# Channel attention with a guessed gate: first gate from 44 rows instead of 135, four slots of 68 rows instead of a ring of 45-row tiles, 512-wide sums, and the first two tiles loaded through two queues

## The chip, the cores and the metric

The kernel runs on one core of a Trainium2 chip. The metric is the device time of one execution in microseconds. The kernel before takes 532.75 us, the median of three runs (532.3 to 534.75).

## The reference

A channel attention of the ECA kind, on an image of 384 x 384 places with 384 channels in bfloat16. Its convolution over channels has the width 1, so the gate of a channel depends on that channel's mean alone:

```python
H = W = 384
C = 384
k = 1
"x": normal(1, H, W, C) * 0.05        # bfloat16
"w1d": normal(k) * 0.05

g = jnp.einsum("bhwc->bc", x) / (H * W)
s = _sigmoid(g * w1d[0])
return x * s[:, None, None, :]
```

The mean needs all of x before the first output could be written. x has 113.25 MB, and so has the output.

## The kernel before

**Tiling.** The 147,456 places are spread over 128 partitions, so that there are 1152 "rows", each of 384 channels in all 128 partitions (128 x 768 bytes). They are cut into 26 tiles, eight of 45 rows and eighteen of 44 (`split(n_rows, TILE)`, TILE = 45). A tile is one DMA in and one DMA out, in which each partition moves one contiguous piece of 45 or 44 x 768 bytes. SBUF holds an arena of rows; a ring hands out places in it, and about six tiles fit at once.

**The guess.** Instead of reading x twice, the kernel guesses the gate. It sums the first three tiles (135 rows), makes the gate `s_early` from their mean, and multiplies and stores every tile with it. Meanwhile it goes on summing. At the end it makes the true gate `s_true` from the sum of everything and compares both as bfloat16 bit patterns. If one channel differs, a second pass reads x again and does everything with `s_true`; if none differs, the output already is what it should be.

**The engines.** Each engine has a list of its own that it works through in order; a small planner records the operations, and adds a semaphore wait wherever one needs another's rows or results.

- SP issues all loads (L91). The load of a tile waits until the stores of the tiles whose place it takes have landed (the wait is at L99).
- PE sums (L206): for each row one matmul of a 128 x 128 block of ones with the row's 384 columns, which adds up over the partitions, and over the rows in one PSUM bank. The sums of the first three tiles are in bank 0, all others in bank 1; bank 2 is for the weight (L183), whose one product is scaled by 1/n twice (L192), for the early and the true mean.
- VectorE copies bank 0 to `total` (L249), and gates tile after tile in place (L165). A gate waits for PE, which must have read the tile.
- ACT loads the weight at the start, makes `s_early` (L255), and then issues all stores (L91), each when its gate is done.
- At the end VectorE adds bank 1 to `total` (L267), ACT makes `s_true` (L273), VectorE compares (L281), reduces (L289) and casts to the flag `redo` (L295). SP, ACT and VectorE read the flag (L326) and skip the second pass or run it. ACT waits last for all stores.

The order around the change is made by one loop over the tiles: before a load is recorded, the tiles that stand in its place are "put" (gate and store), then the load, then the sums; `s_early` is recorded behind the sums of the third tile.

Of the kernel before, what the change touches and what calls it, by code (L numbers as in the profile page):

```python
# [3 lines left out]
P = 128  # L4
ROW = 384
BF16 = mybir.dt.bfloat16
F32 = mybir.dt.float32
U16 = mybir.dt.uint16
I32 = mybir.dt.int32
ACT_F = mybir.ActivationFunctionType  # L10
ALU = mybir.AluOpType


class Planner:
# [9 lines left out]
    def __init__(self, nc, name, n_dma_sems):  # L24
        self.nc = nc
        self.streams = {e: [] for e in ("sync", "scalar", "vector", "tensor", "gpsimd")}
        self.sems = {e: nc.alloc_semaphore(f"{name}_{e}") for e in self.COMPUTE}
        self.count = {e: 0 for e in self.COMPUTE}
        self.pool = [nc.alloc_semaphore(f"{name}_dma_{i}") for i in range(n_dma_sems)]
        self.pool_uses = [0] * n_dma_sems  # L30
        self.n_dma = 0
        self.writer = {}
        self.readers = {}
        self.seen = {e: {} for e in self.streams}
        self.final = []
# [70 lines left out]
def split(n, most):  # L106
    k = -(-n // most)
    return [n // k + (i < n % k) for i in range(k)]


class Ring:


    def __init__(self, size):
        self.size, self.at = size, 0

    def take(self, n):
        if self.at + n > self.size:
            self.at = 0
        self.at += n  # L120
        return self.at - n


TILE = 45
AHEAD_TILES = 3


def bass_standalone__channel_attn_eca__vision_kernel(
# [3 lines left out]
    out: bass.AP,  # L132
):
    B, H, W, C = x.shape
    assert B == 1 and C == ROW and (B * H * W) % P == 0
    n_rows = B * H * W // P
    x_rows, o_rows = x.flatten_outer_dims(), out.flatten_outer_dims()

    def dram(view, r0, n):
        return view[r0 * P : (r0 + n) * P, :].rearrange("(p t) c -> p (t c)", p=P)  # L140

    ones = nc.alloc_sbuf_tensor("ones", [P, P], BF16)
    s_early = nc.alloc_sbuf_tensor("s_early", [P, C], BF16)
    s_true = nc.alloc_sbuf_tensor("s_true", [P, C], BF16)
    w_one = nc.alloc_sbuf_tensor("w_one", [1, 16], BF16)
    w_scaled = nc.alloc_sbuf_tensor("w_scaled", [P, 2], F32)
    warm = nc.alloc_sbuf_tensor("warm", [P, 2], F32)
    wrong = nc.alloc_sbuf_tensor("wrong", [P, 1], F32)
    redo = nc.alloc_sbuf_tensor("redo", [P, 1], I32)
    total = nc.alloc_sbuf_tensor("total", [P, C], F32)  # L150
    n_arena = nc.sbuf_bytes_remaining // (2 * C)
    arena = nc.alloc_sbuf_tensor("arena", [P, n_arena * C], BF16)
    acc = [nc.alloc_psum_tensor(f"acc{i}", [P, 512], F32) for i in range(3)]

    def at(r0, n):
        assert r0 + n <= n_arena
        return arena[:, r0 * C : (r0 + n) * C]

    def rows(r0, n):
        return [("sb", r) for r in range(r0, r0 + n)]  # L160

    def gate(place, n, s):
        s_b = s[:].unsqueeze(1).broadcast_to([P, n, C])
        v = at(place, n).rearrange("p (t c) -> p t c", t=n)
        return lambda e: e.tensor_tensor(v, v, s_b, ALU.mult)  # L165

    sizes = split(n_rows, TILE)
    early_rows = sum(sizes[:AHEAD_TILES])
    plan = Planner(nc, "a", 50)


    plan.op("gpsimd", lambda e: e.memset(warm[:, 0:1], 0.0), writes=["warm"])  # L172
    plan.op("vector", lambda e: e.memset(ones[:], 1.0), writes=["ones"])  # L173
    plan.dma("scalar", w_one[0:1, 0:1], w1d.unsqueeze(0), writes=["w_one"])
    plan.op(
        "scalar",
        lambda e: e.activation(warm[:, 1:2], warm[:, 0:1], ACT_F.Sigmoid),  # L177
        reads=["warm"],
        writes=["warm1"],
    )  # L180
    plan.op(
        "tensor",
        lambda e: e.matmul(  # L183
            acc[2][:, 0:1], ones[0:1, :], w_one[0:1, 0:1], start=True, stop=True
        ),
        reads=["ones", "w_one"],
        writes=["acc2"],
    )
    for i, n in enumerate((early_rows, n_rows)):
        plan.op(  # L190
            "vector",
            lambda e, i=i, n=n: e.tensor_scalar_mul(  # L192
                w_scaled[:, i : i + 1], acc[2][:, 0:1], 1.0 / float(P * n)
            ),
            reads=["acc2"],
            writes=[f"w_scaled{i}"],
        )

    def load(place, n, r0):
        plan.dma("sync", at(place, n), dram(x_rows, r0, n), writes=rows(place, n))  # L200

    def add_rows(place, n, bank, first, last):
        for i in range(n):
            plan.op(
                "tensor",
                lambda e, i=i: e.matmul(  # L206
                    acc[bank][:, :C],
                    ones[:],
                    at(place + i, 1),
                    start=first and i == 0,  # L210
                    stop=last and i == n - 1,
                ),
                reads=["ones"] + (rows(place, n) if i in (0, n - 1) else []),
                writes=[f"acc{bank}"],
                signal=i == n - 1,
            )

    def put(place, n, r0):
        plan.op(
            "vector",  # L220
            gate(place, n, s_early),
            reads=["s_early"] + rows(place, n),
            writes=rows(place, n),
        )
        plan.final.append(
            plan.dma("scalar", dram(o_rows, r0, n), at(place, n), reads=rows(place, n))
        )


    ring = Ring(n_arena)  # L230
    inside = []
    r0 = 0
    for k, n in enumerate(sizes):
        place = ring.take(n)
        while inside and any(
            p < place + n and place < p + m for p, m, _ in inside
        ):
            put(*inside.pop(0))
        load(place, n, r0)
        inside.append((place, n, r0))  # L240
        if k < AHEAD_TILES:
            add_rows(place, n, 0, k == 0, k == AHEAD_TILES - 1)
        else:
            add_rows(place, n, 1, k == AHEAD_TILES, k == len(sizes) - 1)
        r0 += n
        if k == AHEAD_TILES - 1:
            plan.op(
                "vector",
                lambda e: e.tensor_copy(total[:], acc[0][:, :C]),  # L249
                reads=["acc0"],  # L250
                writes=["total"],
            )
            plan.op(
                "scalar",
                lambda e: e.activation(  # L255
                    s_early[:], total[:], ACT_F.Sigmoid, scale=w_scaled[:, 0:1]
                ),
                reads=["total", "w_scaled0", "warm1"],
                writes=["s_early"],
            )  # L260
    for tile in inside:
        put(*tile)


    plan.op(
        "vector",
        lambda e: e.tensor_tensor(total[:], total[:], acc[1][:, :C], ALU.add),  # L267
        reads=["total", "acc1"],
        writes=["total"],
    )  # L270
    plan.op(
        "scalar",
        lambda e: e.activation(  # L273
# [2 lines left out]
        reads=["total", "w_scaled1"],  # L276
        writes=["s_true"],
# [6 lines left out]
        reads=["s_true", "s_early"],  # L284
        writes=["total"],
# [4 lines left out]
        reads=["total"],  # L290
        writes=["wrong"],
# [4 lines left out]
        reads=["wrong"],  # L296
        writes=["redo"],
# [2 lines left out]


    again = Planner(nc, "b", 50)
    ring = Ring(n_arena)
    r0 = 0
    for n in sizes:
        place = ring.take(n)
        again.dma("sync", at(place, n), dram(x_rows, r0, n), writes=rows(place, n))
        again.op(
            "vector",
            gate(place, n, s_true),  # L310
            reads=rows(place, n),
            writes=rows(place, n),
        )
        again.final.append(
            again.dma("scalar", dram(o_rows, r0, n), at(place, n), reads=rows(place, n))
        )
        r0 += n
# [70 lines left out]
```

## Time and profile before

| what | before |
|---|---|
| median of 3 runs | 532.75 us |
| the profiled execution, its own time | 532.74 us |
| its span, from first to last instruction | 530.9 us |
| TensorE busy / VectorE busy | 241.9 / 236.8 us |
| s_early made at | 45.1 us |
| first store issued at | 55.0 us |
| last load issued at | 455.7 us |
| last gate done at | 501.1 us |
| granted TensorE clock, mean | 0.736 |

These are the groups that the change touches. The columns are line, engine, operation, output from inputs, sizes and count, then busy time in us and mean ns of one, then the idle time of the engine just before, and what ended most of it.

```profile
L206 PE MATMUL acc<-arena,ones 128*128 128x384 bf16 x1152 | 241.8, 381 | 248.1 <-DMA arena<-in_x_dram 248.1
L165 DVE TENSOR_TENSOR arena<-arena,s_early 128x16896 bf16<-128x16896 bf16 (+1 forms) x26 | 234.1, 9019 | 222.0 <-PE acc L206 221.3
L249 DVE COPY total<-acc 128x384 f32<-128x384 f32 x1 | 0.6, 557 | 42.1 <-PE acc L206 42.1
L255 ACT ACTIVATE s_early<-total,w_scaled 128x384 bf16<-128x384 f32 x1 | 0.6, 614 | 42.4 <-DVE total L249 42.4
```

And these are the transfers: line, queue, count, size of one, and the median time from its issue to its landing.

```profile
arena<-in_x_dram SPq DMA_DIRECT2D x18, 4224.0 KB, 27.6
out_dram<-arena ACTq DMA_DIRECT2D x18, 4224.0 KB, 73.6
arena<-in_x_dram SPq DMA_DIRECT2D x8, 4320.0 KB, 30.2
out_dram<-arena ACTq DMA_DIRECT2D x8, 4320.0 KB, 58.7
```

PE's idle time is ended by loads and VectorE's by PE: both engines follow the data. A store is on its way for about 3.7 times as long as a turn of 20 us takes, which says that several stores stand in their queue at any time.

### The profile page before, as it was taken

What the parts mean: (1) busy time and instruction counts of PE and PEld (TensorE: products, weight loads), DVE (VectorE), ACT (ScalarE), POOL (GpSimd) and SP (SyncE); (2) the same over time, 40 slices, a digit from 0 to 9 for tenths busy, and PEclk for the clock granted to TensorE, in tenths of its full rate; (3) what the DMA queues carried; (4) which work ended last, traced back from release to release, by engine and by line L of the source; (5) the groups of instructions that cost most, each with busy time, mean ns of one, the idle gap of its engine ahead of it and who ended that gap; (6) DMA issues with size and microseconds to landing.
All of it is one profiled execution on the core that took longest, in us unless ns stands there. A gap on an engine that the chain in (4) does not pass through costs nothing.

```text
span 530.9 us, 2501 instructions
## 1 busy us (share of the span) xinstructions
PE 241.9 (46%) x1153; PEld 127.3 (24%) x1153; DVE 236.8 (45%) x34; ACT 2.7 (1%) x4; POOL 0.3 (0%) x5
## 2 busy tenths in 40 slices
PE   0979643326257256156156266256155265265000
PEld 0435312213123133023033133123033033133000
DVE  0005999561542642642642633642642633633800
ACT  1000000000000000000000000000000000000000
POOL 0000000000000000000000000000000000000000
PEclk9989867588576677686786775686786786676755
DMA  9999999999999999999999999999999999999996
GB/s 372 419 436 437 413 419 440 432 424 442 422 442 422 443 426 438 438 420 444 425 433 446 415 442 440 418 440 437 423 443 428 430 444 415 443 443 414 443 435 290
DMA packets 7502, 226.67 MB, mean 427 GB/s; under 512 B 834, under 2 KB 834, under 8 KB 834
## 3 DMA queue, kind: packets, MB, share of 16 engines
q1 hardware_dynamic: 3744, 113.25, 49.7%
q10 hardware_dynamic: 3746, 113.25, 49.5%
q8 instruction: 9, 0.15, 0.1%
q14 instruction: 3, 0.02, 0.0%
HBM read 113.25 MB, written 113.25 MB: 427 GB/s over the span
## 4 chain that ended last, share of the span: by engine, by line
another core or an unknown queue 63%; DMA 19%; DVE 7%; PE 3%; SPq 1%; issue 1%; ACT 0%; DVEq 0%
DMA arena<-in_x_dram 12%; DMA out_dram<-arena 8%; DVE arena L165 7%; PE acc L206 3%; SPq L91 1%; ACT s_true L273 0%; ACT s_early L255 0%; DVE total L281 0%; DVE total L249 0%; DVE wrong L289 0%; DVE total L267 0%; SPq L99 0%; DVE redo L295 0%; DVEq L99 0%
## 5 line engine op out<-in xcount | busy, mean ns | idle before, releaser
L206 PE MATMUL acc<-arena,ones 128*128 128x384 bf16 x1152 | 241.8, 381 | 248.1 <-DMA arena<-in_x_dram 248.1
L165 DVE TENSOR_TENSOR arena<-arena,s_early 128x16896 bf16<-128x16896 bf16 (+1 forms) x26 | 234.1, 9019 | 222.0 <-PE acc L206 221.3
L206 PEld LDWEIGHTS acc<-arena,ones 128*128 128x128 bf16 x1152 | 127.2, 112 | 362.3 <-DMA arena<-in_x_dram 257.8
L249 DVE COPY total<-acc 128x384 f32<-128x384 f32 x1 | 0.6, 557 | 42.1 <-PE acc L206 42.1
L273 ACT ACTIVATE s_true<-total,w_scaled 128x384 bf16<-128x384 f32 x1 | 0.6, 614 | 455.9 <-DVE total L267 455.9
L177 ACT ACT_TABLE_LOAD x1 | 1.3, 1283 | 1.3 <-PEq L373 1.3
L183 PE MATMUL acc<-w_one,ones 1*128 1x1 bf16 x1 | 0.2, 158 | 2.1 <-DMA w_one<-in_w1d_dram 2.1
L281 DVE TENSOR_TENSOR total<-s_true,s_early 128x384 f32<-128x384 uint16 x1 | 0.6, 559 | 0.7 <-ACT s_true L273 0.7
L255 ACT ACTIVATE s_early<-total,w_scaled 128x384 bf16<-128x384 f32 x1 | 0.6, 614 | 42.4 <-DVE total L249 42.4
L192 DVE TENSOR_SCALAR w_scaled<-acc 128x1 f32<-128x1 f32 x2 | 0.2, 154 | 1.3 <-PE acc L183 1.3
L183 PEld LDWEIGHTS acc<-w_one,ones 1*128 1x128 bf16 x1 | 0.1, 97 | 2.0 <-issue 2.0
L289 DVE TENSOR_REDUCE wrong<-total 128x1 f32<-128x384 f32 x1 | 0.6, 553 | 0.0
L267 DVE TENSOR_TENSOR total<-total,acc 128x384 f32<-128x384 f32 x1 | 0.5, 547 | 0.0
L173 DVE MEMSET ones<- 128x128 bf16 x1 | 0.2, 165 | 0.8 <-PEq L373 0.8
L177 ACT ACTIVATE warm<-warm 128x1 f32<-128x1 f32 x1 | 0.2, 202 | 0.0
L295 DVE CAST redo<-wrong 128x1 int32<-128x1 f32 x1 | 0.2, 154 | 0.0
L373 POOL MEMSET const-bfloat16-1.0<- 128x1 bf16 x1 | 0.1, 103 | 0.0
L373 POOL MEMSET const-uint8-127<- 128x1 uint8 x1 | 0.1, 103 | 0.0
L373 POOL MEMSET const-float32-1.0<- 128x1 f32 x1 | 0.1, 100 | 0.0
L172 POOL MEMSET warm<- 128x1 f32 x1 | 0.1, 99 | 0.3 <-POOLq L373 0.3
L373 POOL MEMSET const-float32-0.0<- 128x1 f32 x1 | 0.1, 99 | 0.2 <-issue 0.2
## 6 DMA issues: line engine op xcount, KB each, us to landing
arena<-in_x_dram SPq DMA_DIRECT2D x18, 4224.0 KB, 27.6
out_dram<-arena ACTq DMA_DIRECT2D x18, 4224.0 KB, 73.6
arena<-in_x_dram SPq DMA_DIRECT2D x8, 4320.0 KB, 30.2
out_dram<-arena ACTq DMA_DIRECT2D x8, 4320.0 KB, 58.7
w_one<-in_w1d_dram ACTq DMA_DIRECT2D x1, 0.0 KB
```

The costliest lines, as they stand in the source:

```text
L91: ("op", lambda e: e.dma_start(out, in_), self.pool[i], 16)
L165: return lambda e: e.tensor_tensor(v, v, s_b, ALU.mult)
L177: lambda e: e.activation(warm[:, 1:2], warm[:, 0:1], ACT_F.Sigmoid),
L183: lambda e: e.matmul(acc[2][:, 0:1], ones[0:1, :], w_one[0:1, 0:1], start=True, stop=True),
L206: lambda e, i=i: e.matmul(acc[bank][:, :C], ones[:], at(place + i, 1), start=first and i == 0, stop=last and i == n - 1,),
L249: lambda e: e.tensor_copy(total[:], acc[0][:, :C]),
L255: lambda e: e.activation(s_early[:], total[:], ACT_F.Sigmoid, scale=w_scaled[:, 0:1]),
L267: lambda e: e.tensor_tensor(total[:], total[:], acc[1][:, :C], ALU.add),
L273: lambda e: e.activation(s_true[:], total[:], ACT_F.Sigmoid, scale=w_scaled[:, 1:2]),
L281: lambda e: e.tensor_tensor(total[:], s_true[:].bitcast(U16), s_early[:].bitcast(U16), ALU.not_equal),
L289: lambda e: e.reduce_max(wrong[:], total[:], axis=mybir.AxisListType.X),
L373: nc = _bacc.Bacc("TRN2", target_bir_lowering=False, num_devices=1)
```

## The change

It has four parts.

1. The early gate is made from the first tile alone, which has 44 rows (EDGE).
2. The ring is replaced by four fixed slots of 68 rows (SLOT). The tiles are one of 44 rows, fifteen of 68, and two of 44 at the end: 18 instead of 26. Tile k stands in slot k mod 4, and its load waits for the store of tile k - 4.
3. A matmul takes 512 columns, a row and a third, instead of 384, and three PSUM banks take turns. Since 512 is 384 + 128, the channels stand shifted by 0, 128 and 256 columns in the three banks; six operations of VectorE add the pieces into `total`, once for the early and once for the full sum.
4. The first two tiles are loaded in two halves by rows, the first half issued by SP and the second by ACT. The loading of the weight moves behind the first tile's load, so that in ACT's list stand: half of tile 0, the weight, `s_early`, half of tile 1, then the stores.

The core of the diff:

```diff
-TILE = 45
-AHEAD_TILES = 3
+WIDE = 512
+EDGE, SLOT = 44, 68
...
-    sizes = split(n_rows, TILE)
-    early_rows = sum(sizes[:AHEAD_TILES])
+    n_slots = n_arena // SLOT
+    full, rest = divmod(n_rows - EDGE, SLOT)
+    if rest < EDGE:
+        full, rest = full - 1, rest + SLOT
+    sizes = [EDGE] + [SLOT] * full + [4 * q for q in split(rest // 4, EDGE // 4)]
...
-    def load(place, n, r0):
-        plan.dma("sync", at(place, n), dram(x_rows, r0, n), writes=rows(place, n))
+    def load(place, n, r0, queues=("sync",)):
+        of = dram(x_rows, r0, n)
+        i = 0
+        for queue, m in zip(queues, split(n, -(-n // len(queues)))):
+            plan.dma(
+                queue,
+                at(place + i, m),
+                of[:, i * C : (i + m) * C],
+                writes=rows(place + i, m),
+            )
+            i += m
...
+    def add_rows(place, n, group, first, last):
+        n_wide = n * C // WIDE
+        start = place * C
+        for i in range(n_wide):
+            bank = acc[group][i % 3]
             plan.op(
                 "tensor",
-                lambda e, i=i: e.matmul(
-                    acc[bank][:, :C],
+                lambda e, i=i, bank=bank: e.matmul(
+                    bank[:, :],
                     ones[:],
-                    at(place + i, 1),
+                    arena[:, start + i * WIDE : start + (i + 1) * WIDE],
...
+    def add_banks(group, copy):
+        for m, lo, hi in ((0, 0, C), (0, C, WIDE), (1, 0, 256), (1, 256, WIDE),
+                          (2, 0, P), (2, P, WIDE)):
+            c = (128 * m + lo) % C
+            part = total[:, c : c + hi - lo]
+            of = acc[group][m][:, lo:hi]
...
-    ring = Ring(n_arena)
     for k, n in enumerate(sizes):
-        place = ring.take(n)
-        while inside and any(
-            p < place + n and place < p + m for p, m, _ in inside
-        ):
+        place = k % n_slots * SLOT
+        if len(inside) == n_slots:
             put(*inside.pop(0))
-        load(place, n, r0)
+        load(place, n, r0, ("sync", "scalar") if k < 2 else ("sync",))
         inside.append((place, n, r0))
-        if k < AHEAD_TILES:
-            add_rows(place, n, 0, k == 0, k == AHEAD_TILES - 1)
+        if k == 0:
+            weight()
+            add_rows(place, n, 0, True, True)
         else:
-            add_rows(place, n, 1, k == AHEAD_TILES, k == len(sizes) - 1)
+            add_rows(place, n, 1, k == 1, k == len(sizes) - 1)
...
-        if k == AHEAD_TILES - 1:
+        if k == 0:
+            add_banks(0, copy=True)
...
+    add_banks(1, copy=False)
```

In the program made from it, PE runs 864 sums where it ran 1152, VectorE 12 adding operations where it ran 2, SP issues 18 loads and ACT 2 where SP issued 26, and ACT issues 18 stores where it issued 26. `weight()` holds the weight's load, the warming of the sigmoid table, the weight's matmul and its two scalings, as they stood at the start before.

More of the change, by code (lines that the diff above doesn't have):

```diff
@@ L108, in split @@
     return [n // k + (i < n % k) for i in range(k)]
[L111 to L121, printed above, removed]
-TILE = 45
-AHEAD_TILES = 3
+WIDE = 512
+EDGE, SLOT = 44, 68
 def bass_standalone__channel_attn_eca__vision_kernel(
@@ L134, in bass_standalone__channel_attn_eca__vision_kernel @@
     B, H, W, C = x.shape
-    assert B == 1 and C == ROW and (B * H * W) % P == 0
+    assert B == 1 and C == ROW and (B * H * W) % (4 * P) == 0
     n_rows = B * H * W // P
@@ L152, in bass_standalone__channel_attn_eca__vision_kernel @@
     arena = nc.alloc_sbuf_tensor("arena", [P, n_arena * C], BF16)
-    acc = [nc.alloc_psum_tensor(f"acc{i}", [P, 512], F32) for i in range(3)]
+    acc = [
+        [nc.alloc_psum_tensor(f"acc{g}_{i}", [P, WIDE], F32) for i in range(3)]
+        for g in range(2)
+    ]
+    w_all = nc.alloc_psum_tensor("w_all", [P, WIDE], F32)
     def at(r0, n):
@@ L165, in gate @@
         return lambda e: e.tensor_tensor(v, v, s_b, ALU.mult)
-    sizes = split(n_rows, TILE)
-    early_rows = sum(sizes[:AHEAD_TILES])
+    n_slots = n_arena // SLOT
[3 more added lines that the diff above has]
+    sizes = [EDGE] + [SLOT] * full + [4 * q for q in split(rest // 4, EDGE // 4)]
+    assert sum(sizes) == n_rows and max(sizes) <= SLOT
     plan = Planner(nc, "a", 50)
@@ L173, in bass_standalone__channel_attn_eca__vision_kernel @@
     plan.op("vector", lambda e: e.memset(ones[:], 1.0), writes=["ones"])
[L174 to L197, printed above, removed]
-    def load(place, n, r0):
-        plan.dma("sync", at(place, n), dram(x_rows, r0, n), writes=rows(place, n))
-    def add_rows(place, n, bank, first, last):
-        for i in range(n):
+    def load(place, n, r0, queues=("sync",)):
[9 more added lines that the diff above has]
+            i += m
@@ L204, in add_rows @@
+    def add_rows(place, n, group, first, last):
[3 more added lines that the diff above has]
+            bank = acc[group][i % 3]
             plan.op(
                 "tensor",
-                lambda e, i=i: e.matmul(
-                    acc[bank][:, :C],
+                lambda e, i=i, bank=bank: e.matmul(
+                    bank[:, :],
                     ones[:],
-                    at(place + i, 1),
-                    start=first and i == 0,
-                    stop=last and i == n - 1,
-                ),
@@ L213, in add_rows @@
-                reads=["ones"] + (rows(place, n) if i in (0, n - 1) else []),
-                writes=[f"acc{bank}"],
-                signal=i == n - 1,
-            )
+                    arena[:, start + i * WIDE : start + (i + 1) * WIDE],
+                    start=first and i < 3,
+                    stop=last and i >= n_wide - 3,
+                ),
+                reads=["ones"] + (rows(place, n) if i in (0, n_wide - 1) else []),
+                writes=[f"acc{group}"],
+                signal=i == n_wide - 1,
+            )
@@ new lines, in add_banks @@
+    def add_banks(group, copy):
[4 more added lines that the diff above has]
+            of = acc[group][m][:, lo:hi]
+            if copy and (m, lo) == (0, 0):
+                emit = lambda e, part=part, of=of: e.tensor_copy(part, of)
+            else:
+                emit = lambda e, part=part, of=of: e.tensor_tensor(
+                    part, part, of, ALU.add
+                )
+            plan.op("vector", emit, reads=[f"acc{group}", "total"], writes=["total"])
@@ L227, in put, with weight @@
         )
-    ring = Ring(n_arena)
+    def weight():
+        plan.dma("scalar", w_one[0:1, 0:1], w1d.unsqueeze(0), writes=["w_one"])
+        plan.op(
+            "scalar",
+            lambda e: e.activation(warm[:, 1:2], warm[:, 0:1], ACT_F.Sigmoid),
+            reads=["warm"],
+            writes=["warm1"],
+        )
+        plan.op(
+            "tensor",
+            lambda e: e.matmul(
+                w_all[:, 0:1], ones[0:1, :], w_one[0:1, 0:1], start=True, stop=True
+            ),
+            reads=["ones", "w_one"],
+            writes=["w_all"],
+        )
+        for i, n in enumerate((sizes[0], n_rows)):
+            plan.op(
+                "vector",
+                lambda e, i=i, n=n: e.tensor_scalar_mul(
+                    w_scaled[:, i : i + 1], w_all[:, 0:1], 1.0 / float(P * n)
+                ),
+                reads=["w_all"],
+                writes=[f"w_scaled{i}"],
+            )
     inside = []
@@ L233, in bass_standalone__channel_attn_eca__vision_kernel @@
     for k, n in enumerate(sizes):
-        place = ring.take(n)
-        while inside and any(
-            p < place + n and place < p + m for p, m, _ in inside
-        ):
+        place = k % n_slots * SLOT
+        if len(inside) == n_slots:
             put(*inside.pop(0))
-        load(place, n, r0)
+        load(place, n, r0, ("sync", "scalar") if k < 2 else ("sync",))
         inside.append((place, n, r0))
-        if k < AHEAD_TILES:
-            add_rows(place, n, 0, k == 0, k == AHEAD_TILES - 1)
+        if k == 0:
+            weight()
+            add_rows(place, n, 0, True, True)
         else:
-            add_rows(place, n, 1, k == AHEAD_TILES, k == len(sizes) - 1)
+            add_rows(place, n, 1, k == 1, k == len(sizes) - 1)
         r0 += n
-        if k == AHEAD_TILES - 1:
[L247 to L252, printed above, removed]
+        if k == 0:
+            add_banks(0, copy=True)
             plan.op(
@@ L262, in bass_standalone__channel_attn_eca__vision_kernel @@
         put(*tile)
[L265 to L270, printed above, removed]
+    add_banks(1, copy=False)
     plan.op(
@@ L302, in bass_standalone__channel_attn_eca__vision_kernel @@
     again = Planner(nc, "b", 50)
-    ring = Ring(n_arena)
     r0 = 0
-    for n in sizes:
-        place = ring.take(n)
+    for k, n in enumerate(sizes):
+        place = k % n_slots * SLOT
         again.dma("sync", at(place, n), dram(x_rows, r0, n), writes=rows(place, n))
```

## The prediction

> **What bounds the kernel now.** I read four views in this order: the busy shares by engine, the 40 slices, the chain of waits, and a table of stages. The first two say what is not the bound and what is.
>
> ```profile
> PE 241.9 (46%) x1153; PEld 127.3 (24%) x1153; DVE 236.8 (45%) x34; ACT 2.7 (1%) x4; POOL 0.3 (0%) x5
> ...
> DMA  9999999999999999999999999999999999999996
> GB/s 372 419 436 437 413 419 440 432 424 442 422 442 422 443 426 438 438 420 444 425 433 446 415 442 440 418 440 437 423 443 428 430 444 415 443 443 414 443 435 290
> ...
> HBM read 113.25 MB, written 113.25 MB: 427 GB/s over the span
> ```
>
> TensorE and VectorE idle more than half of the span; the 16 DMA engines are at nine tenths or more in every slice but the last. Each byte goes in once and out once, so there was one pass. The table of stages (microseconds, busy time of PE, PEld, DVE, ACT, POOL, granted clock, DMA share, GB/s) shows how flat the rate is:
>
> ```profile
> 5.00:45.00 40.00, 26.46 (x135) 14.28 (x135) 0.45 (x1) 0.00 (x0) 0.00 (x0) 0.96 1.02 438
> 45.00:60.00 15.00, 11.65 (x61) 6.40 (x62) 14.32 (x3) 0.61 (x1) 0.00 (x0) 0.89 1.01 415
> 60.00:80.00 20.00, 10.72 (x49) 5.51 (x48) 20.00 (x3) 0.00 (x0) 0.00 (x0) 0.75 0.98 422
> 100.00:480.00 380.00, 179.55 (x838) 93.73 (x838) 168.31 (x20) 0.00 (x0) 0.00 (x0) 0.72 1.00 433
> 480.00:525.00 45.00, 8.76 (x44) 4.72 (x44) 13.29 (x6) 0.61 (x1) 0.00 (x0) 0.61 1.01 433
> 525.00:531.00 6.00, 0.00 (x0) 0.00 (x0) 0.00 (x0) 0.00 (x0) 0.00 (x0) 0.50 0.29 124
> ```
>
> Loads alone (5 to 45), both directions (100 to 480) and stores alone (480 to 525) run at one rate within the counting error of whole packets. So it does not matter when stores begin: 226.5 MB at 433 GB/s are 523 us, and only gaps, overhead per packet and the two ends can be changed. Of the chain, one turn suffices:
>
> ```profile
> 375.76 0.02 issue
> 375.77 0.02 SPq L99
> 375.79 0.03 issue
> 375.82 0.33 SPq L91
> 376.15 19.58 another core or an unknown queue
> ```
>
> SP waits for a store to land (L99), issues the next load (L91), and waits 19.6 us for the next store: a turn of 19.97 us moves 88 rows (a row being 128 x 768 bytes), 0.227 us a row. Stores are far behind when they are issued (median 73.6 us to landing), so the store queue never empties and no engine's slowness is seen.
>
> The DMA packet records of the same trace give finer numbers. A packet of 33,792 bytes starts 1.247 us after the one before on its engine, one of 34,560 bytes 1.275 us: 768 bytes cost 28.2 ns, so a packet has about 4.9 ns that don't grow with it, and a packet followed by a semaphore write costs 6 ns more. With both queues filled, load and store packets alternate one for one. A transfer that joins a queue waits for about three packets already taken (the first store, issued at 54.98, first moves at 59.42); on idle engines the first packet comes 1.0 us after the issue (0.73 to 1.73), and the first packets take about 2.2 us, not 1.28. The engines drift apart: the last store lands between 526.37 and 530.39, a spread of 4.0 us. Beside the 1.4 us steps of the drift lie instruction fetches, nine of 16 KB.
>
> **What the Trainium skill says.** DMA: Bandwidth & Descriptors, section "Issuing engines are not separate DMA queues": transfers from several engines run on the same 16 DMA engines and interleave, and a second issuer saves only the time of issuing. Its section "Queues, rings and completion order" has the engines take turns between queues, a packet each; the one-for-one alternation agrees. TensorE: Matmul & The Clock Gate, section "Wait — 56ns, not 53.3ns?": a 512-wide matmul starts every 426.7 ns cold and 215.7 ns warm; here 384 columns go at 320 ns cold and 166 ns warm, the same price per column. Runtime: NRT & Kernel Launch, section "Instruction fetch mechanics": instructions come in blocks of 16 KiB, 256 each; 1153 matmuls with as many weight loads are 2306 instructions, nine blocks, as the trace has.
>
> **The change part by part.** *Matmuls.* 864 of 512 columns for 1152 of 384: the same columns, so PE keeps about 242 us and stays hidden. It drops 576 instructions with the weight loads, so seven fetches for nine. A fetch holds one DMA engine about 1.4 us, and counts only if that engine ends last: between -2.8 and 0 us.
>
> *Tiles.* 18 for 26. Per DMA engine there were 26 x 2 x 8 = 416 packets; now 18 stores and 16 whole loads x 8, and two loads in halves x 16, make 304. 112 x 4.9 ns = 0.55 us, with 14 fewer semaphore writes 0.63 us saved. The packets grow to 52,224 bytes, a size the trace lacks; above it I take the same slope. If it were 1% worse the whole would be 5 us slower; two sizes with one slope speak against it, so I keep nothing of that.
>
> *Start.* Tile 0 is 22 rows on SP and 22 on ACT, at once, sharing the engines: 44 rows, 10 us, landed at about 13, as the 45 rows of before. The weight's two bytes now queue behind ACT's half and cost 1 us more, since the matmul of the weight stands ahead of tile 0's on PE: start at 14.5. 33 matmuls partly cold, about 9.8 us as tile 0 took before: 24.3. Instead of one copy (0.56) VectorE makes six moves out of PSUM, 384, 128, 256, 256, 128 and 384 columns wide. At the 0.55 us for 384, of which 0.15 is fixed (the one-column operations), they come to 2.4 us; with waits 2.7. With the sigmoid's 0.61 s_early stands at about 27.7, not 45.8. All of this is beside loads already issued.
>
> On ACT the second half of tile 1's load is issued only behind s_early, at 27.8, and store 0 behind that. Tile 1 is therefore complete only at about 55: 34-row packets alternating with SP's 68-row packets, after three taken packets. PE needs 13.7 us (51 matmuls, the first 5 us cold), VectorE 26,112 columns at 8.96 us per 16,896, 13.8: store 1 comes at about 83 and can move at 84. Store 0 comes at 37, after 9 us of gate.
>
> *First gap.* Until load 4 may be issued there are four loads and store 0: 44 + 68 x 3 + 44 = 292 rows, 66.3 us, to 69.0. As a store packet of 44 rows alternates with a load packet of 68, the loads finish first and store 0 last. Load 4 waits for exactly that store, and store 1 is not gated: all engines are dry. Cost: 0.1 from landing to SP, 1.0 to the first packet, and the slow restart, about 0.6: +1.7 us. In before, six slots hid this, since load 5 and stores 0 and 1 overlapped. Bounds: 0 (if stores got equal bytes, not equal packets) and 2.5.
>
> *Second gap.* Load 4 alone takes 15.4 us, to about 86; store 1 can move at 84. Taken as nothing, with 2 us of margin. If it is missed, the engines wait for gate 1: up to 2.4 us and a restart.
>
> *Steady state.* A turn is 136 rows, 30.9 us, a slot's round 123. Load 31 to 38, PE 13.7, gate 13.8, store 31, waits 3: at most 100. Spare are about 25 us, so four slots do not starve the queues: 0.
>
> *Tail.* When the last load lands, about 95 rows of stores are before its own: 21.5 us. PE 10, gate 9, issue 1 make 20. Taken as nothing; margin 1.5 us. The check behind it grows from one sum of 0.55 us to six of 2.4 and would now end about 10 us before the stores: hidden.
>
> *Drift.* The slowest engine's 4.0 us were there by 95 us. The first gap makes all wait for the slowest at 69 (about 1.2 us late by then) and then start together; I take another 2.5 us by the end with fewer fetches. 3.7 for 4.0: -0.3.
>
> *Sum.* The profiled execution took 532.74 us (span 530.87 and 1.87 around it), which is the median of the runs to 0.01. 532.74 - 0.63 + 1.7 - 0.3 = 533.5.
>
> **The rivals.** *A second gap* (slower): gate 1 comes later than load 4 ends. For it: the ACT half of tile 1 hangs on s_early, and one step of the alternation is 3.2 us, more than the margin. Against: the margin is there by each duration I have. It decides when s_early is later than about 30 us. 533.5 + 2.4 + 0.4 = 536.3.
>
> *No gap and less drift* (faster): store 0 lands while load 3 runs, and two fetches fewer halve the drift. 532.74 - 0.63 - 2.0 = 530.1. For it: every fetch is worth 1.4 us on its engine. Against: the one-for-one alternation.
>
> *Four slots or the tail fall short*: each turn waits, or the last gate misses its margin. A wait of 0.5 us in each of 13 turns gives 540. Against: 25 us of spare.
>
> *The second pass runs*, as 5,632 values in a mean for 17,280 before might round the gate otherwise: another 523 us, 1,057. Against: inputs of deviation 0.05 have means near 0.05 / 75 = 0.0007, times a weight near 0.05: the gate is off 0.5 by some 0.00001, where bfloat16 rounds away 0.001.
>
> **How the numbers follow.** One gap, 0.60, at 533.5 (531.5 to 535.3); two gaps 0.24 at 536.3; no gap 0.10 at 530.1; short slots or tail 0.05; second pass 0.01. 0.5% is 2.7 us, about what a measurement can tell. Faster (under 530.1) is half of the third case: 0.05. Slower (over 535.4) is most of the second, the fourth and fifth, and the edge of the first: 0.28. Within it 0.67. The range goes from 530.6 to 537.0.
>
> **What would show it.** Right: DMA share below 9 in the slice around 69 us, no dip in the steady state, load 4 issued just as store 0 lands, s_early near 28, store 1 issued before 85, spread of the last landings under 4 us. Wrong: a second dip near 86; dips in every turn; a rate other than 433 in the steady state, which would say that packet size has a price; HBM traffic doubled.

## The result, and the profile after

The changed kernel takes 537.85 us, the median of six runs (536.58 to 540.61), where the kernel before takes 532.83 (six runs, 532.3 to 534.75). The ratio is 1.0094, with a 95% interval from 1.0066 to 1.0122: about 5 us slower, and above the predicted range, which ends at 537.0. Some executions of five of the kernels tried below took 4 to 11 us longer than the others of the same kernel (in the three of these that were profiled the parts of the last load landed 14 to 15 us apart on the 16 DMA engines), and the ratios leave out those more than 1.5% above the fastest.

The profiled execution took 538.78 us. Its page, with the busy shares, the slices of the DMA engines, and the traffic:

```profile
span 536.9 us, 1879 instructions
...
PE 220.9 (41%) x848; PEld 91.8 (17%) x865; DVE 239.7 (45%) x36; ACT 2.7 (1%) x4; POOL 0.3 (0%) x5
...
DMA  8999979999999999999999999999999999999987
GB/s 355 465 436 436 396 301 428 425 436 432 436 424 428 428 428 433 436 436 428 436 433 436 436 436 436 436 436 429 432 436 412 436 429 423 432 427 413 439 377 329
...
HBM read 113.25 MB, written 113.25 MB: 422 GB/s over the span
```

TensorE and VectorE are as idle as before (some matmul records are missing: 848 of 865), and each byte still goes once, so the second pass didn't run. Two places have changed. The sixth slice, 67 to 81 us, has a 7 for DMA and 301 GB/s, and the last but one falls to 377 where before had 435.

Three of the stages that the prediction shows of before, and then three finer ones (columns as there: busy time of PE, PEld, DVE, ACT, POOL, clock, DMA share, GB/s):

```profile
60.00:80.00 20.00, 19.90 (x92) 9.07 (x93) 12.09 (x1) 0.00 (x0) 0.00 (x0) 1.00 0.88 361
100.00:480.00 380.00, 155.21 (x595) 64.55 (x607) 174.11 (x13) 0.00 (x0) 0.00 (x0) 0.72 1.00 431
480.00:525.00 45.00, 17.36 (x62) 6.82 (x61) 19.14 (x6) 0.00 (x0) 0.00 (x0) 0.69 0.97 410
...
69.00:73.00 4.00, 3.95 (x19) 1.76 (x18) 4.00 (x1) 0.00 (x0) 0.00 (x0) 1.00 0.67 204
73.00:82.00 9.00, 8.95 (x42) 4.12 (x42) 9.00 (x2) 0.00 (x0) 0.00 (x0) 1.00 0.88 377
515.00:525.00 10.00, 0.00 (x0) 0.00 (x0) 9.90 (x5) 0.00 (x0) 0.00 (x0) 0.58 0.86 372
```

The three finer ones in before:

```profile
69.00:73.00 4.00, 0.00 (x0) 0.00 (x0) 4.00 (x1) 0.00 (x0) 0.00 (x0) 0.61 0.96 415
73.00:82.00 9.00, 7.72 (x30) 3.94 (x31) 9.00 (x2) 0.00 (x0) 0.00 (x0) 0.61 1.01 434
515.00:525.00 10.00, 0.00 (x0) 0.00 (x0) 0.00 (x0) 0.00 (x0) 0.00 (x0) 0.50 1.00 433
```

The long stage from 100 to 480 runs at 431 GB/s for 433. What is missing lies around 69 (204 GB/s for 415, then 377 for 434) and between 515 and 525 (372 for 433). From 69 to 73 TensorE is busy throughout at the full clock: it is summing tile 1, late. A turn in the steady state, in the chain of waits:

```profile
319.84 0.33 SPq L91
320.16 30.42 another core or an unknown queue
...
350.65 0.33 SPq L91
```

It takes 30.8 us for a 68-row tile in and one out, 0.227 us a row as before, so bigger packets have no price; by the packet records one of 52,224 bytes takes 1.925 us, where the slope of the smaller ones gives 1.922. The early part of the chain shows the order that empties the queue:

```profile
26.76 27.14 DMA arena<-in_x_dram
...
54.04 5.96 PE acc L188 x15
...
60.05 7.73 PE acc L188 x35
...
67.91 10.93 DVE arena L156
```

ACT issues its half of tile 1 at 26.76, behind `s_early`. That half lands at 53.91, 13.7 us of matmuls follow, and gate 1 starts only at 67.91 and ends at 81.67. Meanwhile SP waits for store 0, as the timeline of SP from 60 us on shows (start, length, operations run together):

```profile
71.44 36.39 SPq L91 DMA_DIRECT2D arena<-in_x_dram  x2
```

Load 4 is issued at 71.44, just after store 0 has landed (71.36). Until then the DMA engines are dry, that is, without a packet to move: by the packet records the last packet of store 0 ends between 69.35 and 70.87 us, depending on the engine, and the first of load 4 starts at 72.4. At the other end the chain runs over the last tile's work:

```profile
471.22 33.64 DMA arena<-in_x_dram
...
504.91 6.25 PE acc L188 x17
...
511.21 3.42 PE acc L188 x15
...
514.72 8.96 DVE arena L156
```

The last load lands at 504.86 and its store is issued at 523.7, 18.8 us later. The stores ahead of it had ended between 521.7 and 526.4, depending on the DMA engine: most engines were dry again, 1.8 us on average.

The DMA packet records give an account of the whole. For each of the 16 engines I add up how much later each packet starts than its predecessor's size allows (28.2 ns per 768 bytes and 4.9 ns). A second profiled execution of the changed kernel, from a later sitting, took 536.87 us and lies nearer to the usual time; both are shown, in us more than before, averaged over the engines:

| term | predicted | profiled, 538.78 | second, 536.87 |
|---|---|---|---|
| fewer packets (computed) | -0.6 | -0.6 | -0.6 |
| dry stretch from 68 to 80, with restart | +1.7 | +3.8 | +3.7 |
| slow packets from 80 to 100 | 0 | +1.1 | +1.1 |
| dry stretch at the end, from 518 on | 0 | +1.9 | +1.0 |
| all the rest | 0 | +1.3 | +0.4 |
| last landing, later than the mean engine | -0.3 | -1.5 | -1.5 |
| sum | +0.8 | +6.0 | +4.1 |

The last landing came at 530.39 us before, at 536.36 and 534.45 after: +6.0 and +4.1.

### The profile page after: what moved, and what is told of

It is laid out like the page before. It is cut to its first block, busy times and chain, and to the rows that moved or that the text cites. A ratio compares the mean times of both kernels' runs of the same rounds, so it can differ in the third digit from the quotient of the medians.

```text
span 536.9 us, 1879 instructions
## 1 busy us (share of the span) xinstructions
PE 220.9 (41%) x848; PEld 91.8 (17%) x865; DVE 239.7 (45%) x36; ACT 2.7 (1%) x4; POOL 0.3 (0%) x5
## 4 chain that ended last, share of the span: by engine, by line
another core or an unknown queue 62%; DMA 21%; DVE 7%; PE 6%; issue 1%; SPq 1%; ACT 0%; ACTq 0%; DVEq 0%
DMA arena<-in_x_dram 11%; DMA out_dram<-arena 7%; DVE arena L156 6%; PE acc L188 6%; DMA w_one<-in_w1d_dram 3%; DVE total L210 1%; SPq L91 1%; ACT s_true L285 0%; DVE total L208 0%; DVE total L293 0%; DVE wrong L301 0%; ACTq L91 0%; SPq L99 0%; PE w_all L237 0%
## 5 line engine op out<-in xcount | busy, mean ns | idle before, releaser
L156 DVE TENSOR_TENSOR arena<-arena,s_early 128x26112 bf16<-128x26112 bf16 (+1 forms) x18 | 233.1, 12958 | 263.9 <-PE acc L188 263.2
L188 PE MATMUL acc<-arena,ones 128*128 128x512 bf16 x847 | 220.7, 425 | 278.7 <-DMA arena<-in_x_dram 276.0
L188 PEld LDWEIGHTS acc<-arena,ones 128*128 128x128 bf16 x864 | 91.7, 108 | 407.3 <-DMA arena<-in_x_dram 252.4
L210 DVE TENSOR_TENSOR total<-total,acc 128x128 f32<-128x128 f32 (+2 forms) x11 | 4.5, 408 | 0.3
## 6 DMA issues: line engine op xcount, KB each, us to landing
arena<-in_x_dram ACTq DMA_DIRECT2D x1, 2112.0 KB, 12.7
```

Source lines behind the costliest of these rows:

```text
L188: lambda e, i=i, bank=bank: e.matmul(bank[:, :], ones[:], arena[:, start + i * WIDE : start + (i + 1) * WIDE], start=first and i < 3, stop ...
L210: emit = lambda e, part=part, of=of: e.tensor_tensor(part, part, of, ALU.add)
```

## The experiments

The theory is that the queues run dry in two places, each for a reason that can be taken away. The first is at 69 us: the ACT half of tile 1 behind `s_early` makes store 1 late, and with four slots load 4 has only store 0 to wait for. The second is at the end, where the last tile's sums and gate outlast the stores ahead. The rivals: that a smaller early gate or a second queue is itself the cost; that tiles of 68 rows are, in every turn; that the wide sums are.

Each kernel below is a change to the changed kernel, unless it says that it starts from before.

**Tile 1 by SP alone.** Only tile 0 is loaded in halves.

```diff
-load(place, n, r0, ("sync", "scalar") if k < 2 else ("sync",))
+load(place, n, r0, ("sync", "scalar") if k < 1 else ("sync",))
```

> The changed kernel with tile 1 loaded whole by SP; only tile 0 still goes in halves. Theory A (the dry stretch near 69 us, made by tile 1 being complete only at 54 us because its ACT half is issued behind s_early): tile 1 lands near 29, store 1 is issued near 57, no dry stretch, and the whole of its price goes: the 3.8 us of the stretch with its slow restart and the 1.1 us at the second start of the stores near 85. 533 us, +-1. Theory B (large packets or four slots cost something in every turn): the stretch goes but the time stays at 536 or more. Theory C (the end: the last gate comes late): 536 to 537, as the end is untouched.

Measured: 532.82 us (530.46 to 540.38, 14 runs), ratio 0.9998 (0.9974 to 1.0021). In the timeline of VectorE gate 1 now starts at 39.93:

```profile
39.93 13.76 DVE L156 TENSOR_TENSOR arena<-arena,s_early 128x26112 bf16<-128x26112 bf16 x1 [1.36 <-PE acc L188]
```

It ends at 53.7, so store 1 stands in the queue well before store 0 lands. Its window from 69 to 73 us:

```profile
69.00:73.00 4.00, 0.00 (x0) 0.00 (x0) 4.00 (x1) 0.00 (x0) 0.00 (x0) 0.50 0.97 418
```

418 GB/s for 204: the dry stretch is gone, and with it the whole loss against before in the median (the profiled execution took 530.57 us, one of the shortest). Taking one half-load out of ACT's list is enough, with four slots and the early gate as they were. Whether it is the half's place in that list or the second queue, this run doesn't tell.

**Six slots of 44 rows, and the same with tile 1 by SP.** The first keeps ACT's half behind `s_early`; the tiles become 27.

```diff
-EDGE, SLOT = 44, 68
+EDGE, SLOT = 44, 44
```

> The changed kernel with SLOT = 44: six slots and 27 tiles (44 x 25, 28, 24), halves and all else as in the change. Theory A: tile 1 still lands late, near 46, but its sums and gate take 19 us, not 27, and six slots give 308 rows of work, to about 72 us, ahead of the first awaited store: store 1 is issued near 65 and there is no dry stretch. 533 us +-1.5. If theory B (packet size in every turn) holds, also about 533, so this tells A and B apart only together with e1. If the 512-wide sums or the early gate cost by themselves: 537 to 538.

> Six slots of 44 rows, early gate, wide sums, and only tile 0 in halves. Theory A: as the run with slots of 44 rows, neither dry at the start nor late at the end: 531.8 us, +-0.7.

Measured: 532.1 us for the first (531.37 to 534.34, 14 runs), ratio 0.9995 (0.9983 to 1.0006), and 532.1 for the second (531.45 to 533.51, 21 runs), ratio 0.9989 (0.9982 to 0.9995). In the first, `s_early` stands at 26.7 us and ACT issues its half then, as in the changed kernel, yet the window from 69 to 73 has 406 GB/s:

```profile
69.00:73.00 4.00, 4.00 (x20) 1.82 (x19) 4.00 (x2) 0.00 (x0) 0.00 (x0) 1.00 0.94 406
```

So the late half alone is not the loss: it costs when it meets four slots of 68 rows. The run changes the number of slots and the length of the tiles together (the half has 22 rows for 34, and its tile's sums and gate are shorter), so which of the two saves it is not shown.

**ACT's half of tile 1 first.** It is recorded before the weight and `s_early`; the kernel was run in two sittings.

```diff
-        load(place, n, r0, ("sync", "scalar") if k < 2 else ("sync",))
+        if k != 1:
+            load(place, n, r0, ("sync", "scalar") if k < 1 else ("sync",))
         if k == 0:
+            load(SLOT, sizes[1], n, ("sync", "scalar"))
             weight()
```

> The changed kernel with both tiles still in halves on both queues, but ACT issues its half of tile 1 ahead of the weight and of s_early. Theory A: what costs is the place of the ACT half in ACT's list, not the use of two queues: tile 1 lands near 22 to 29, no dry stretch near 69, 533 us +-1. Rival D (two queues for loads cost by themselves): as the changed kernel, 537 to 538.

> The kernel with ACT's half of tile 1 ahead of s_early again, on another chip, since its times lay far apart. Theory A: no dry stretch; the load queue alone is empty from 63 to 72 us while stores run, with two slow restarts. 533 to 535 us. Theory D (two queues for the loads cost): 537.

Measured: 537.43 us (532.17 to 543.91, 21 runs), ratio 1.0061 (1.0038 to 1.0083), then 535.62 (533.82 to 543.4, 6 runs), ratio 1.0041 (1.0027 to 1.0055). A miss: the time of before did not come back. In the second sitting's profile (536.66 us) the stretch at 69 is full, and another is half empty:

```profile
69.00:73.00 4.00, 4.00 (x21) 1.78 (x19) 4.00 (x1) 0.00 (x0) 0.00 (x0) 1.00 0.96 413
516.00:524.00 8.00, 0.00 (x0) 0.00 (x0) 7.83 (x7) 0.00 (x0) 0.00 (x0) 0.60 0.45 190
```

The edit moves more than was meant: the weight's two bytes now queue behind 34 rows, so `s_early` comes at 44.4 us for 26.75. And the last load is slow to land, in the chain of the same profile:

```profile
467.47 35.42 DMA arena<-in_x_dram
```

It was issued 3.8 us earlier than in the changed kernel and landed 2.0 earlier (502.89 for 504.86), but the stores ahead of its own ended 5 to 6 us earlier: the engines stood still for 5.3 us on average at the end. What was saved at 69 was given back there. The 16 engines drift apart in this kernel: the parts of load 4 land 1.6 us apart and those of the last load 6.8, where the changed kernel has 2.4 and 3.7.

**The same with a short last tile.** The last 88 rows go as 48, 24 and 16.

```diff
-sizes = [EDGE] + [SLOT] * full + [4 * q for q in split(rest // 4, EDGE // 4)]
+sizes = [EDGE] + [SLOT] * full + [48, 24, 16]
```

> The kernel with ACT's half of tile 1 ahead of s_early and with the last 88 rows in tiles of 48, 24 and 16. Theory A with C: the 5.3 us for which the engines of that kernel stood dry at its end go, 531 to 532.5 us. Theory D (two queues for the loads cost by themselves): still 535 or more, without a dry stretch at either end.

Measured: 537.63 us (531.39 to 541.24, 22 runs), ratio 1.0047 (1.0025 to 1.0069). A miss too, so a shorter last tile alone does not mend the end of that kernel. In its profile, of an execution of 541.15 us, the parts of the last load land 15.4 us apart on the 16 engines, against 2.6 us for load 4. So the last load was late whatever the length of its tile. Why some engines fall behind there was not found.

**ACT's half of tile 1 behind store 0.** Here ACT's half of tile 1 goes behind gate 0 and store 0:

```diff
         place = k % n_slots * SLOT
+        if k == 1:
+            put(*inside.pop(0))
```

> The changed kernel with the suspected wait made longer: ACT issues its half of tile 1 behind store 0 instead of ahead of it. Worked out from alternating packets: tile 1 complete near 77, store 1 issued near 105, all engines dry from about 84 to 105.5. Theory A (dry time adds to the whole one for one): 21 us and a restart over a kernel without a dry stretch: 554 us, +-2.5. Rival (some of the wait is made up later, since the queues then are fuller): under 550.

Measured: 558.44 us (555.35 to 561.32, 6 runs), ratio 1.0485 (1.0458 to 1.0512). The window of the dry stretch:

```profile
84.00:109.00 25.00, 25.00 (x113) 11.18 (x112) 14.48 (x2) 0.00 (x0) 0.00 (x0) 0.96 0.01 3
```

That is 3 GB/s for 25 us. By the packet records an engine was dry for 24.2 us on average. The first packets behind the stretch are those of store 1, and they are not slow (0.04 us). What is slow, by 1.5 us, are the packets from 130 to 134 us, when the next load begins beside the stores, as SP's timeline shows:

```profile
127.21 0.33 SPq L91 DMA_DIRECT2D arena<-in_x_dram  x1
```

The end costs 2.2. The last landing is 25.6 us later than in before (556.01 for 530.39), so almost all of this dry stretch is paid and not won back later.

**Before, with the gate from five tiles.** A dry stretch made in the other kernel, without slots, halves or wide sums.

```diff
-AHEAD_TILES = 3
+AHEAD_TILES = 5
```

> The kernel before, with AHEAD_TILES = 5, so a dry stretch without any other part of the change: the early gate waits for five tiles of 45 rows, store 0 comes near 75, the sixth load ends near 64, the engines are dry for about 11.4 us. Theory A: 532.6 + 11.4 + 1 = 545 us, +-1.5. Rival (what costs in the change is not the dry stretch, so it is made up here): 533 to 535.

Measured: 545.18 us (543.72 to 545.53, 5 runs), ratio 1.0233 (1.022 to 1.0246). The window, and ACT's timeline:

```profile
63.00:77.00 14.00, 9.67 (x59) 5.41 (x57) 11.10 (x3) 0.61 (x1) 0.00 (x0) 0.99 0.14 58
```

```profile
65.82 0.61 ACT L255 ACTIVATE s_early<-total,w_scaled 128x384 bf16<-128x384 f32 x1 [63.04 <-DVE total L249]
75.65 9.40 ACTq L91 DMA_DIRECT2D out_dram<-arena  x2
```

The arena is full before the first store can go at 75.65. By the packet records 12.3 us are dry. Again the first packets behind are a store's and not slow (0.01 us), and 1.2 us are lost from 88 to 94 us, when the next load, issued at 87.43, begins beside the stores. The kernel is 12.7 us slower. The cost of such a stretch doesn't hang on the rest of the change.

**Before, with the early gate alone.**

```diff
-AHEAD_TILES = 3
+AHEAD_TILES = 1
```

> The kernel before with one part of the change alone: the early gate from the first tile (45 rows) instead of the first three. Theory A: the engines are never dry in it, so nothing is gained or lost by earlier stores: 532.7 us +-1, with the first store issued near 36 instead of 55. A rival in which earlier mixing of loads and stores costs: 534 or more.

Measured: 533.49 us (532.15 to 542.25, 14 runs), ratio 1.003 (1.0005 to 1.0056). Its profile is of the longest of these executions, so no stage is read from it. The early gate alone saves nothing, which fits a rate that doesn't care whether stores run. By the interval it even costs 0.3 to 3 us, of which the cause is not shown; it is not the 5 us of the change.

**Before, with the wide sums alone.** The 512-wide matmuls and the pieced sums go into the kernel before, with tiles that divide by four.

```diff
-sizes = split(n_rows, TILE)
+sizes = [44] * 24 + [48] * 2
...
-        for i in range(n):
+        n_wide = n * C // 512
+        for i in range(n_wide):
+            bank = acc[group][i % 3]
```

> The kernel before with one part alone: 512-wide sums into shifted banks and their six adds, twice, in tiles of 44 rows (two of 48), with the early gate from three tiles and all loads on SP as before. Theory A (only dry DMA engines cost): the sums are hidden, seven instruction fetches instead of nine: 532.2 us, from 531.2 to 533.0. Rival (the wide sums or the six adds cost): 534 or more.

Measured: 531.41 us (531.2 to 531.84, 13 runs), ratio 0.998 (0.9972 to 0.9988): about 1.1 us faster than before, and the lowest median of all kernels here. Its queue of instruction fetches, on the page:

```profile
q8 instruction: 7, 0.11, 0.1%
```

With 865 matmuls for 1153 there are seven fetches for nine. PE is busy 239.2 us for 241.9 and hidden, so the matmuls' own time isn't what is saved. That it is the two fetches was argued in the prediction; no run separates them from the rest of this edit.

**The changed kernel again, with a short last tile, and with both repairs.** The first is the changed kernel as it is. The second has the sizes 48, 24 and 16 at the end, the third also tile 1 by SP alone.

> The changed kernel itself on the same chip as these, for its spread. Theory A: median 537 to 538, dry stretch near 69 us of 2.5 to 3.5 us in its profile, a slow restart near 72 and another near 85. Theory C (the end): the time changes from run to run with the moment at which the last load lands on the slowest DMA engine.

> The changed kernel with its last 88 rows as tiles of 48, 24 and 16 rows, not two of 44, so that the last gate is done about 6 us, not 1.5, before the stores ahead of it end. Theory C as a part beside A (in the repeat of the change the last store landed 13.5 us after the fastest engine's store before it, where 8 packets take 10.0: the last gate came late by about 1.3 us): 535.8 us, 1 to 1.5 less than the changed kernel. If the end is covered, as the prediction took it: no change, 537 to 538. If A is wrong and the end is the main price: 533 to 534.

> Both repairs: tile 1 whole on SP and the last 88 rows in tiles of 48, 24 and 16. Theory A with C: 531.3 us, +-0.8, under the kernel before by what the fewer packets and instruction fetches save; no dry stretch at 69 us and none at the end.

Measured: 536.93 us (535.29 to 539.86, 6 runs), ratio 1.0084 (1.0062 to 1.0107); 536.19 (536.07 to 536.75, 5 runs), ratio 1.0068 (1.0055 to 1.0081); 531.87 (530.58 to 538.11, 22 runs), ratio 1.0 (0.998 to 1.002). The first lies just inside the predicted range, as the six runs above lie just outside. Its window at 69 repeats that of the changed kernel:

```profile
69.00:73.00 4.00, 4.00 (x21) 1.77 (x19) 4.00 (x1) 0.00 (x0) 0.00 (x0) 1.00 0.64 204
```

And this is the end of the second, in its windows:

```profile
515.00:525.00 10.00, 5.20 (x12) 1.64 (x12) 3.29 (x2) 0.00 (x0) 0.00 (x0) 0.67 0.95 411
```

411 GB/s for 372. Summing and gating 16 rows takes 8.7 us instead of 18.8, and the packet records have 0.02 us lost after 518 us, for 1.0 and 1.9. By the ratios the short tile gains 0.9 us on the repeat and 1.4 on the first six runs, which agrees, though the intervals overlap. Their spread shrinks from 4 us and more to 0.7. From the second to the third the dry stretch at 69 goes, and with it 3.6 us by the ratios or 4.3 by the medians; the records of the second have 3.65 us from 68 to 80 and 1.32 from 80 to 100, those of the third 0.79 and 0.09, which lie where load 4 begins beside the stores and not in a dry stretch.

## Why the prediction was wrong, step by step

**What held.** The place and the cause were named: load 4 is issued at 71.44, when store 0 has landed, and the engines are dry around 69. The times on the way there came within 1.5 us: `s_early` at 26.75 (27.7; its six moves, by the prediction's own figures 2.5 us and not 2.4, took 2.7), store 0 at 36.39 (37), tile 1 complete at 53.9 (55), store 1 issued at 81.7 (83). There is no second gap: load 4 still ran when store 1 came. The steady state has neither waits nor a price of packet size (431 GB/s, turns of 30.8 us for 30.9), the traffic did not double, the matmuls and the redo check stayed hidden, and there are seven fetches.

**The term that failed most: "First gap", +1.7 us, measured 3.7 to 3.8.** The mechanism was right and the size was not: the upper bound was 2.5. The prediction added 0.1 from landing to SP, 1.0 to the first packet, and 0.6 for the restart. The first two held (0.08 and about 1.1), and the restart was 0.8. What it left out of this term is the wait for the slowest engine. The parts of store 0 land between 69.71 and 71.36 on the 16 engines, the last one on an engine that had an instruction fetch at 68.3 (0.93 us in its record; the engine lost 1.3 by it), and SP goes on only behind the last. On average an engine stood idle 2.94 us. Of these only 1.1 are what the prediction counted; 1.3 are the wait for the slowest engine, and 0.5 go from the end of its last packet (70.87) to its landing (71.36). It did say that all wait for the slowest, "about 1.2 us late by then", but put that under "Drift", as if a wait for the slowest were repaid at the end.

**A cost that has no term: the start of store 1.** From 80 to 100 us the packets lose 1.1 us, around 84.8, when store 1 begins beside the loads. The same loss stands in before at 40 to 60 us (0.77 us), when its first stores begin, and in the changed kernel at store 0 (0.68). As the queue empties between stores 0 and 1, the changed kernel pays it twice, 1.8 us in all; where store 1 is already waiting (tile 1 by SP) it is 1.2 in all, and 0.01 from 80 to 100. The prediction took this start for a wait of three packets alone, without a loss.

**"Tail", taken as nothing with a margin of 1.5 us, measured 1.0 and 1.9.** Its 20 us from the last load to its store were 18.8. But of the stores ahead it counted 95 rows, 21.5 us, by working out where each would stand; in the trace they lasted 16.8 to 21.5 us by engine, and only the slowest engine had as much as counted. The short last tile shows it: with it the loss is 0.02. A part of this loss does not reach the time, as the next term gives it back: the last landing of the second profile is only 0.65 us later than with the short tile (534.45 for 533.80).

**"Drift", -0.3, measured -1.5.** The last landing is 3.1 us later than the mean of the engines' last packets before, and 1.6 us in both executions of the changed kernel. The prediction had the first gap bring the engines together. It is the dry stretch at the end that does: the last store but one still lands 4.7 us apart on the engines of the first profile, and the last 1.4; and with the short last tile, which keeps the stretch at 69, the last landing is 2.8 us later than the mean again. So the sign was right by luck, and the term gives back a part of what "Tail" cost. It is the one term that erred on the other side.

**"Tiles", -0.63,** is in the packet records as computed, 304 packets for 416. "Matmuls" was kept inside the drift; alone it is worth -1.1 (0.998), inside its bounds of -2.8 and 0.

Of the rivals, "A second gap" at 536.3 and "Four slots or the tail fall short" at 540 stand on either side of the time. The first did not occur as a gap; at its place only the 1.1 us of slow packets are lost. The second is half right: no turn waits in the steady state, but the tail does miss its margin. Its chance of 0.05 was too low for a margin of 1.5 us that rested on a count of rows.

**Left open.** What makes single executions of several kernels long. Where such a one was profiled (ACT's half first, early gate alone), some DMA engines were far behind the others; why was not found. The extra time of ACT's half first over tile 1 by SP is therefore not shown to be a price of the second queue. What is left over in the profiled execution, 1.3 us, contains slow loads near 411 and 494 us, of which the second has less; it was not followed further.

## What to carry to other kernels

When the DMA engines are the bound, look for every moment at which the next transfer can be issued only after the last one in flight has landed, and price it with the wait for the slowest engine, the issue and, where loads come first, a slow restart: here 3.8 us and another 1.1 when the other direction began anew, for a gap whose issue and first packet alone take 1.1. A half of an early tile that stands behind a computed value in its queue delays everything built on that tile; with six slots of 44 rows such a half cost nothing that the times show, with four of 68 about 4 us. At the end, compare the last tile's sums and gate with the stores ahead on the fastest engine; a short last tile was worth about 1 us here.

## What the runs showed of the hardware that was not expected

Two kinds of packets were slow. The first are load packets that come first after idle engines: 0.35 to 1.2 us longer on each engine at 72.4 us. The second are the packets in flight when one direction joins the other: 0.64 to 1.3 us are lost when stores begin beside loads, in before too, and 0.8 to 1.5 when loads begin beside stores (with both repairs, with the gate from five tiles, and with the half behind store 0). A dry stretch by itself doesn't make the next packets slow: where a store ended it, after 12.3 and 24.2 us, the first packets lost 0.01 and 0.04 us.

The end of the kernel decides how far apart the engines end. The last packets of the 16 engines end 3.9 us apart before, 1.4 and 0.35 us apart in the two executions of the changed kernel, and 3.3 us apart with the short last tile, where the end is no longer dry.
